# Idle TensorE matmuls before the last V block and between the transfers of wo, wo's last rows in two strips, and stores of two rows

## The chip, the cores and the metric

The kernel runs on one core of a Trainium2 chip. The metric is the device time of one execution in microseconds, as the median of several runs. A profile of one execution shows what each engine did: TensorE (PE; its weight loads apart as PEld), VectorE (DVE), ScalarE (ACT), GpSimd (POOL) and SyncE (SP), with the DMA engines.

## What is computed

One decode step for one token: attention over a cached K and V, and a gated feed-forward network, mixed by a gate. Cut to what matters:

```python
q = (x @ wq).reshape(1, 1, 32, 128)           # x: 512 values
k, v = each of 8 cached heads (32768 x 128) repeated for 4 query heads
p = softmax(q k^T * 128 ** -0.5)
a = (p v).reshape(1, 1, 4096) @ wo            # wo: 4096 x 512
b = (silu(x @ w_gate) * (x @ w_up)) @ w_down  # 1792 wide
g = sigmoid((x * gate_w).sum())
out = g * a + (1 - g) * b                     # 512 values
```

All inputs are bfloat16. K and V are 64 MB each and are read once.

## The kernel before

**Tiling.** G is 8 cached heads, with HPG = 4 query heads each. The 32768 positions of a head fall into NB = 2 blocks of 16384; a block of K or of V is one page of SBUF, 128 partitions by 128 rows by 128 values, 4 MB. Four pages hold two K and two V blocks (`PG_K`, `PG_V`); a fifth, `PG_X`, holds wq first and wo (32 rows of 512 per partition, seen as `wo_v`) later.

**The main loop on TensorE** (L518) runs G + 1 times. In iteration i, for each block b, `emit_k` transposes the K block of head i (L392, into the PSUM tiles `pst`, copied to `ktT` by VectorE at L671) and computes its scores (L404); `emit_v` multiplies the V block of head i - 1 with the exponentials that ScalarE wrote (L448). A V block is 32 matmuls of 512 columns and 16 output rows; they go to four strips of 32 columns of the array in turn (`32 * c`), so that four stand side by side. `emit_reduce` (L430) adds up what the previous head left in `acc`. The iterations' bounds are told by `pe.If`, so the last iteration has no K part: it does V block 0 of the last head, waits for V block 1 (page 3) and does it, and then runs `emit_end`.

**The end** (`emit_end`): the sums of the exponentials (L483), the last `emit_reduce` as soon as ScalarE has copied `ps_o` to `acc` (L560), then the down projection (14 rows of `wd`) by `emit_wide`: one matmul of 512 columns and one output row per row of the weight, in four strips of `ps_w` (L460). VectorE meanwhile scales and transposes the attention output (L700, L707), TensorE permutes it (L498), and VectorE copies it to `O2` (L709). Then the 32 rows of wo follow, in pieces cut at `WO_CUTS = [0, 8, 18, 26, 31, 32]`, each with a semaphore of its own transfer. The first 18 rows (`WIDE`) are `emit_wide` again. After piece 1 VectorE copies the four strips of `ps_w` to `part` (L711). The later rows use `emit_rows`: four matmuls of 128 columns each, one for each quarter of the output, to partitions 0, 32, 64 and 96 of `ps_c` (L471). After piece 2 `emit_rows` takes `part` with a column of ones at four partitions (`sel4`) as weights, which adds up the strips. At the end VectorE casts `ps_c` to `res_row` (L713), and SyncE and ScalarE store two quarters each, one DMA per quarter (`store`, L206).

**The order of transfers** is written out by hand on SyncE's queue: K and V pages as they come free (L298 to L302 and L281), V block 0 of the last head, wo's piece 0, V block 1 of the last head, `wd`, then wo's pieces 1 to 4 (L319). GpSimd waits for the stores at the end.

**Constants.** VectorE makes `sel4` from `ident` near the start, each step chained on a semaphore (`dchain`); TensorE waits for `N_SEL` of these before the main loop.

Of the kernel before, what the change touches and what calls it, by code (L numbers as in the profile page):

```python
# [6 lines left out]
ALU = mybir.AluOpType  # L7
AX = mybir.AxisListType
BF16 = mybir.dt.bfloat16
# [4 lines left out]
def bass_gated_mix__gqa_block_cached__swiglu_ffn__decode_kernel(  # L14
# [39 lines left out]
    STEP = 16  # L54
# [1 line left out]
    SCALE = float(DH) ** -0.5  # L56
    assert UPG == STEP == 4 * HPG and UPP % NKT == 0 and UPP % NST == 0
    assert KC * H * DH <= PAGE and 2 * KC * F <= PAGE and WOJ * NOUT <= PAGE
    WO_CUTS = [0, 8, 18, 26, 31, 32]
    WIDE = WO_CUTS[2]  # L60
    OC = NOUT // 128

    RQ = 4
    N_SEL = 12
    NSTRIP = 4
    assert RQ * HPG <= 32 and RQ * DH == 512

    PG_K = (0, 2)
# [5 lines left out]
    with ExitStack() as es:  # L74
# [35 lines left out]
        sem_dve_oT1 = S_("s_dve_oT1")  # L110
        sem_dve_oT2 = S_("s_dve_oT2")
        sem_dve_O2 = S_("s_dve_O2")
        sem_dve_row = S_("s_dve_row")
        sem_psw = S_("s_psw")
        sem_pe_w = S_("s_pe_w")
# [48 lines left out]
        nbias = T("nbias", [128, G, HPG], FP32)  # L164
        esum = T("esum", [128, G, NB, HPG], FP32)
        esum2 = T("esum2", [128, G, HPG], FP32)
        sel4 = T("sel4", [128, 16], FP32)
        acc = T("acc", [128, RQ, DH], FP32)
        oT = T("oT", [128, (G + 2) * STEP], FP32)
        rS = T("rS", [128, H], FP32)  # L170
# [1 line left out]
        oTs = T("oTs", [128, H], BF16)  # L172
        O2a = T("O2a", [128, WOJ], BF16)
        O2 = T("O2", [128, WOJ], BF16)
        part = T("part", [128, NOUT], FP32)
        res_row = T("res_row", [128, 128], BF16)

# [15 lines left out]
        ps_e = pst[0][:, 0:512]  # L193
        ps_c = pst[1][:, 0:512]
        ps_w = pst[0][:, 512:1024]

        def row_view(p):
            return page[:, p, :].rearrange("p (r d) -> p r d", d=DH)
# [3 lines left out]
        wo_v = page[:, PG_X, 0 : WOJ * NOUT].rearrange("p (j n) -> p j n", j=WOJ)  # L202

        def store(eng, k):
            for c in (2 * k, 2 * k + 1):
                eng.dma_start(  # L206
                    out[0, :, 128 * c : 128 * (c + 1)], res_row[32 * c : 32 * c + 1, :]
                ).then_inc(sem_out, 16)

        with nc.Block("main") as block:  # L210
            @block.gpsimd
            def _(pool):
                pool.memset(ones_bf[:, :], 1.0).then_inc(sem_const, 1)
                pool.memset(ones_f[:, :], 1.0).then_inc(sem_const, 1)
                npool = [0]

                def chain(ins):
                    ins.then_inc(sem_pool, 1)
                    npool[0] += 1
                    pool.wait_ge(sem_pool, npool[0])  # L220

                chain(pool.memset(ident[:, :], 0.0))
                pool.affine_select(
                    out=ident[:, :],
                    in_=ident[:, :],
                    compare_op=ALU.not_equal,
                    fill=1.0,
                    base=0,
                    pattern=[[-1, 128]],
                    channel_multiplier=1,  # L230
                ).then_inc(sem_ident, 1)
                chain(pool.memset(ident_f[:, :], 0.0))
                pool.affine_select(
                    out=ident_f[:, :],
                    in_=ident_f[:, :],
                    compare_op=ALU.not_equal,
                    fill=1.0,
                    base=0,
                    pattern=[[-1, 128]],
                    channel_multiplier=1,  # L240
                ).then_inc(sem_ident, 1)
                chain(pool.memset(perm[:, :, :], 0.0))
                for e in range(2):
                    pool.affine_select(
                        out=perm[:, e, :],
                        in_=perm[:, e, :],
                        compare_op=ALU.not_equal,
                        fill=1.0,
                        base=-e,
                        pattern=[[0, 2], [-2, 64]],  # L250
                        channel_multiplier=1,
                    ).then_inc(sem_ident, 1)
                pool.iota(
                    colidx[:, :],
                    pattern=[[1, 128]],
                    base=0,
                    channel_multiplier=0,
                    allow_small_or_imprecise_dtypes=True,
                ).then_inc(sem_iota, 1)
                pool.iota(  # L260
                    kf[:, :],
                    pattern=[[1, 1]],
                    base=0,
                    channel_multiplier=1,
                    allow_small_or_imprecise_dtypes=True,
                ).then_inc(sem_iota, 1)
                pool.wait_ge(sem_dve_gpart, 1)
                pool.partition_all_reduce(gtot[:, :], gpart[:, :], 128, ReduceOp.add).then_inc(
                    sem_gtot, 1
                )  # L270
                for g in range(G):
                    pool.wait_ge(sem_pmax, STEP * (g + 1))
                    pool.partition_all_reduce(  # L273
                        gmax[:, g, :], pmax[:, g * STEP : g * STEP + HPG], 128, ReduceOp.max
                    ).then_inc(sem_gmax, 1)
                pool.wait_ge(sem_out, 64)

            @block.sync
            def _(sp):
# [54 lines left out]
            def _(pe):  # L334
# [132 lines left out]
                    )  # L467

                def emit_rows(lhs, rhs, first, last):
                    for oc in range(OC):  # L470
                        ins = pe.matmul(  # L471
                            ps_c[32 * oc : 32 * oc + 1, 0:128],
                            lhs,
                            rhs[:, oc * 128 : (oc + 1) * 128],
                            start=first,
                            stop=last,
                            skip_group_check=True,
                        )
                    return ins

                def emit_end():
                    pe.wait_ge(sem_dve_esum2, 1)
                    pe.matmul(  # L483
                        ps_e[:, 0:H],
                        ones_f[:, :],
                        esum2[:, :, :].rearrange("p g h -> p (g h)"),
                        start=True,
                        stop=True,
                    ).then_inc(sem_pe_S, 1)
                    emit_reduce((G + 1) * STEP)  # L490
                    pe.wait_ge(sem_dve_tT, 1)
                    pe.wait_ge(sem_ld_wd, 16)
                    pe.wait_ge(sem_psw, 1)
                    for j in range(FC):
                        emit_wide(wd, tT, j, j < NSTRIP, False)
                    pe.wait_ge(sem_dve_oT2, 1)
                    pe.wait_ge(sem_dve_pm, 1)
                    pe.matmul(  # L498
                        ps_m[:, M_O0 : M_O0 + WOJ], pmat[:, :], O2a[:, :], start=True, stop=True
                    ).then_inc(sem_pe_O2, 1)  # L500
                    pe.wait_ge(sem_dve_O2, 1)
                    for k, s in enumerate(sem_wo):
                        pe.wait_ge(s, 16)
                        for j in range(WO_CUTS[k], WO_CUTS[k + 1]):
                            if j < WIDE:
                                ins = emit_wide(wo_v, O2, j, False, j >= WIDE - NSTRIP)
                            else:
                                ins = emit_rows(
                                    O2[:, j : j + 1], wo_v[:, j, :], j == WIDE, j == WOJ - 1
                                )  # L510
                        if k == 1:
                            ins.then_inc(sem_pe_w, 1)
                        if k == 2:
                            pe.wait_ge(sem_dve_w, 1)
                            emit_rows(sel4[:, 0:1], part[:, :], False, False)
                    ins.then_inc(sem_pe_sum, 1)

                with pe.Fori(0, (G + 1) * STEP, STEP) as i:  # L518
                    for b in range(NB):
                        with pe.If(i < G * STEP):  # L520
                            emit_k(i, b)
                        with pe.If(i > 0):
                            emit_v(i, b)
                    with pe.If(i > (G - 1) * STEP):
# [48 lines left out]
            def _(dve):  # L573
# [39 lines left out]
                )  # L613
                dve.tensor_copy(pmat[:, :], pmat_f[:, :]).then_inc(sem_dve_pm, 1)
                dve.wait_ge(sem_ident, 1)
                dchain(dve.tensor_copy(sel4[:, :], ident[:, 0:16]))
                for c in range(1, NSTRIP):
                    dchain(
                        dve.tensor_tensor(
                            sel4[:, :], sel4[:, :], ident[:, 32 * c : 32 * c + 16], ALU.add  # L620
                        )
                    )
                assert ndc[0] == N_SEL + 1
# [83 lines left out]
                dve.transpose(O2a[:, :], oTs[:, :]).then_inc(sem_dve_oT2, 1)  # L707
                dve.wait_ge(sem_pe_O2, 1)
                dve.tensor_copy(O2[:, :], ps_m[:, M_O0 : M_O0 + WOJ]).then_inc(sem_dve_O2, 1)  # L709
                dve.wait_ge(sem_pe_w, 1)  # L710
                dve.tensor_copy(part[:, :], ps_w[:, :]).then_inc(sem_dve_w, 1)  # L711
                dve.wait_ge(sem_pe_sum, 1)
                dve.tensor_copy(res_row[:, :], ps_c[:, 0:128]).then_inc(sem_dve_row, 1)  # L713


# [26 lines left out]
```

## Time and profile before

| what | us |
|---|---|
| median of 3 runs | 353.63 (353.47 to 353.99) |
| the profiled execution's own time | 354.17 |
| its span, from the first instruction to the last | 352.4 |
| last matmul group ends, cast to `res_row` starts | 349.96, 349.99 |
| stores are issued from | 350.31 |
| TensorE busy | 269.4 (76%) |
| VectorE busy | 178.5 (51%) |
| mean DMA rate over the span | 421 GB/s |

A row of the profile names an engine, a line of the kernel (L448 is line 448) and an operation with its output and inputs; "x32" is the number of instructions, "128x512" partitions by elements. "PEclk" is the share of the full TensorE clock that was granted. A wait is put down to what ended it. The chain of work follows what ended last back from the end of the span. TensorE's matmuls overlap, and their ends are modelled, so lengths of single ones hold their way through the array as well as their columns.

### The profile page before, as it was taken

The numbers are of one execution on the slowest core, as the hardware profiler recorded it, in microseconds if no ns is written. First come the engines' busy times: TensorE is split into PE (matmuls) and PEld (weight loads), VectorE is DVE, ScalarE is ACT, GpSimd is POOL, SyncE is SP. The second block draws the span as 40 slices with busy tenths as digits, with TensorE's granted clock in tenths as the row PEclk, the third lists the DMA queues.
The fourth block names the chain that finished last, engine by engine and source line by source line (L and its number), as shares of the span: only waits on it lengthen the run. The fifth ranks groups of instructions, "written<-read, shape, count | busy, mean of one in ns | idle before, by whom it ended". The sixth has DMA issues, their size and how long they took to land.

```text
span 352.4 us, 8926 instructions
## 1 busy us (share of the span) xinstructions
PE 269.4 (76%) x4005; PEld 231.1 (66%) x4005; DVE 178.5 (51%) x204; ACT 32.3 (9%) x148; POOL 5.8 (2%) x24
## 2 busy tenths in 40 slices
PE   0446986997999959697798959795997859695376
PEld 0446976976687949395786849494966759593033
DVE  0310967655683938266562828274655728193001
ACT  1000000400120040002100040003000030004000
POOL 0200000000000000000000000000000000000000
PEclk9999988789898998769885978679887969898656
DMA  8999999999999999999999999999999999999994
GB/s 331 411 432 426 445 433 416 430 424 450 420 432 424 450 421 428 424 450 420 432 424 450 420 432 424 450 420 432 424 450 420 432 424 450 420 432 420 439 402 163
DMA packets 5924, 148.23 MB, mean 421 GB/s; under 512 B 666, under 2 KB 796, under 8 KB 924
## 3 DMA queue, kind: packets, MB, share of 16 engines
q1 hardware_dynamic: 5912, 148.12, 98.2%
q8 instruction: 6, 0.10, 0.1%
q14 instruction: 2, 0.02, 0.0%
q10 hardware_dynamic: 4, 0.00, 0.0%
HBM read 148.11 MB, written 0.00 MB: 420 GB/s over the span
## 4 chain that ended last, share of the span: by engine, by line
DMA 58%; PE 36%; DVE 3%; issue 1%; SPq 1%; ACT 0%; ACTq 0%
DMA page<-in_A_k_cache_dram 54%; PE pst L392 25%; PE ps_sc L404 6%; DMA page<-in_A_v_cache_dram 5%; PE ps_o L448 3%; DVE ktT L671 3%; PE pst L460 1%; PE ps_m L430 1%; PE pst L471 1%; SPq L302 0%; ACT acc L560 0%; SPq L298 0%; SPq L299 0%; DVE res_row L713 0%; SPq L300 0%
## 5 line engine op out<-in xcount | busy, mean ns | idle before, releaser
L671 DVE COPY ktT<-pst 128x2048 bf16<-128x2048 bf16 x128 | 155.8, 1224 | 106.6 <-PE pst L392 99.6
L392 PE MATMUL pst<-ident_f,page 128*128 128x128 f32 x1024 | 158.2, 311 | 41.5 <-DMA page<-in_A_k_cache_dram 39.2
L392 PEld LDWEIGHTS pst<-ident_f,page 128*128 128x128 f32 x1024 | 134.6, 161 | 53.0 <-DMA page<-in_A_k_cache_dram 47.0
L404 PEld LDWEIGHTS ps_sc<-qcur,ktT 128*128 128x128 bf16 x2048 | 67.1, 97 | 11.4 <-DVE ktT L671 10.0
L404 PE MATMUL ps_sc<-qcur,ktT 128*128 128x8 bf16 x2048 | 67.9, 166 | 8.6 <-DVE ktT L671 8.6
L448 PE MATMUL ps_o<-page,ET 128*16 128x512 bf16 x512 | 43.0, 495 | 7.9 <-DMA page<-in_A_v_cache_dram 7.9
L448 PEld LDWEIGHTS ps_o<-page,ET 128*16 128x16 bf16 x512 | 13.5, 105 | 26.7 <-issue 20.3
L539 ACT ACTIVATE nbias<-gmax 128x4 f32<-128x4 f32 x8 | 1.6, 205 | 263.2 <-POOL gmax L273 263.2
L548 ACT ACTIVATE ET<-ps_sc,nbias 128x128 bf16<-128x128 f32 x64 | 24.1, 553 | 0.7
L548 ACT ACTIVATION_READ_ACCUMULATOR ET<-ps_sc,nbias 128x1 f32 x64 | 18.1, 282 | 0.0
L676 DVE TENSOR_REDUCE pmaxf<-ps_sc 128x4 f32<-128x512 f32 x16 | 11.1, 692 | 11.5 <-PE ps_sc L404 11.5
L430 PE MATMUL ps_m<-sel,acc 128*128 128x4 f32 x72 | 11.4, 282 | 3.7 <-ACT acc L560 3.7
L430 PEld LDWEIGHTS ps_m<-sel,acc 128*128 128x128 f32 x72 | 10.8, 229 | 4.3 <-ACT acc L560 4.3
L340 PE MATMUL ps_m<-ones_bf,x_row 1*128 1x1 bf16 x4 | 0.3, 172 | 13.6 <-DMA gw_row<-in_gate_w_dram 13.6
L377 PE MATMUL ps_m<-xT,page 128*128 128x1 bf16 x112 | 6.9, 198 | 4.2 <-DMA page<-in_B_w_up_dram 4.2
L377 PEld LDWEIGHTS ps_m<-xT,page 128*128 128x128 bf16 x112 | 6.8, 159 | 4.3 <-DMA page<-in_B_w_up_dram 4.3
L340 PEld LDWEIGHTS ps_m<-ones_bf,x_row 1*128 1x128 bf16 x4 | 0.2, 114 | 13.6 <-DMA gw_row<-in_gate_w_dram 13.6
L694 DVE RECIPROCAL rS<-pst 128x32 f32<-128x32 f32 x1 | 0.4, 358 | 15.3 <-PE pst L483 15.3
L273 POOL PARTITION_ALL_REDUCE gmax<-pmax x8 | 3.0, 372 | 291.7 <-DVE pmax L678 291.7
L560 ACT ACTIVATE acc<-ps_o 128x512 f32<-128x512 f32 x8 | 5.2, 650 | 17.0 <-PE ps_o L448 17.0
L585 DVE CAST xT<-ps_m 128x4 bf16<-128x4 f32 x1 | 0.2, 163 | 12.5 <-PE ps_m L340 12.5
L353 PE MATMUL ps_m<-xT,page 128*128 128x1 bf16 x128 | 3.6, 165 | 0.3 <-DVE gwT L586 0.3
(68 smaller groups left out, 33.6 us busy)
## 6 DMA issues: line engine op xcount, KB each, us to landing
page<-in_A_k_cache_dram SPq DMA_DIRECT2D x16, 4096.0 KB, 26.9
page<-in_A_v_cache_dram SPq DMA_DIRECT2D x16, 4096.0 KB, 31.2
page<-in_A_wq_dram SPq DMA_DIRECT2D x1, 4096.0 KB, 12.4
page<-in_A_wo_dram SPq DMA_DIRECT2D x2, 1024.0 KB, 24.7
page<-in_B_w_gate_dram SPq DMA_DIRECT2D x1, 1792.0 KB, 15.7
page<-in_B_w_up_dram SPq DMA_DIRECT2D x1, 1792.0 KB, 20.5
wd<-in_B_w_down_dram SPq DMA_DIRECT2D x1, 1792.0 KB, 20.5
page<-in_A_wo_dram SPq DMA_DIRECT2D x1, 1280.0 KB, 23.1
```

The lines of the kernel that those rows point to most:

```text
L353: ins = pe.matmul(ps_m[:, M_Q0 + h : M_Q0 + h + 1], wq_v[:, c, h * DH : (h + 1) * DH], xT[:, c : c + 1], start=(c == 0), stop=(c == KC - 1),)
L377: ins = pe.matmul(ps_m[:, base + j : base + j + 1], wgu[:, w, c, :].rearrange("d (p j) -> d j p", j=FC)[:, j, :], xT[:, c : c + 1], start= ...
L392: ins = pe.transpose(pst[u % NST][:, k * 128 : (k + 1) * 128], kv[:, n * 128 : (n + 1) * 128], ident_f[:, :],)
L404: ins = pe.matmul(ps_sc[b][:, col : col + 2 * HPG], kt[:, k, e, :], qcur[:, e, :], start=(e == 0), stop=(e == 1),)
L430: ins = pe.matmul(ps_m[:, M_P0 : M_P0 + HPG], acc[:, q, :], sel4[:, q * HPG : (q + 1) * HPG], start=(q == 0), stop=(q == RQ - 1),)
L448: ins = pe.matmul(ps_o[32 * c : 32 * c + RQ * HPG, :], ET[:, n : n + RQ, :].rearrange("p n h -> p (n h)"), view[:, k * RQ : (k + 1) * RQ, ...
L460: return pe.matmul(ps_w[32 * c : 32 * c + 1, :], vec[:, j : j + 1], w[:, j, :], start=first, stop=last, skip_group_check=True,)
L471: ins = pe.matmul(ps_c[32 * oc : 32 * oc + 1, 0:128], lhs, rhs[:, oc * 128 : (oc + 1) * 128], start=first, stop=last, skip_group_check=True,)
L548: act.activation(ET[:, b * R : (b + 1) * R, h], sc[:, h, :], ACT.Exp, bias=nbias[:, g, h : h + 1], scale=SCALE, accum_out=esum[:, g, b, h ...
L560: act.activation(acc[:, :, :].rearrange("p q d -> p (q d)"), ps_o[:, :], ACT.Copy).then_inc(sem_acc, STEP)
L671: dve.tensor_copy(ktT[:, u % NKT, :], pst[u % NST][:, :].bitcast(BF16)).then_inc(sem_cp, 1)
L676: dve.tensor_reduce(pmaxf[:, b, :], sc, AX.X, ALU.max).then_inc(sem_pmax, 4)
```

## The change

Before V block 1 of the last head TensorE runs 18 matmuls (`NWARM`) of the identity with 512 columns of `ktT` into a part of `pst` that nobody reads (`ps_d`); they stand in a loop with two in its body, within a `pe.If` that is true in the last iteration alone. Six such matmuls stand behind wo's piece 1 and two behind piece 2 (`NGAP`). wo's cuts move to 30 and 32 at the end, and rows 18 to 25 become wide (`WIDE` is 26). `part` is copied after piece 2, and its sum starts the accumulation in `ps_c`. The rows from 26 on and `part` use two strips of two output rows: the weight is two columns wide, one of them zero (`O2z`, `sel5`), so quarter `oc` lands in row `oc % 2` of strip `oc // 2`. `res_row` then has its rows at partitions 0, 1, 32 and 33, and each queue stores two of them with one DMA. VectorE zeroes `O2z` and a column of `sel5` at the start and fills `O2z` with two copies after `O2`.

```diff
-    WO_CUTS = [0, 8, 18, 26, 31, 32]
-    WIDE = WO_CUTS[2]
+    WO_CUTS = [0, 8, 18, 26, 30, 32]
+    KW = 2
+    WIDE = WO_CUTS[KW + 1]
+    NWARM = 18
+    NGAP = [0, 6, 2]
...
-    N_SEL = 12
+    N_SEL = 13
     NSTRIP = 4
+    RPS = 2
...
+        ps_d = pst[1][:, 512:1024]
...
         def store(eng, k):
-            for c in (2 * k, 2 * k + 1):
-                eng.dma_start(
-                    out[0, :, 128 * c : 128 * (c + 1)], res_row[32 * c : 32 * c + 1, :]
-                ).then_inc(sem_out, 16)
+            n = RPS * 128
+            eng.dma_start(
+                out[0, 0, n * k : n * (k + 1)].rearrange("(c n) -> c n", c=RPS),
+                res_row[32 * k : 32 * k + RPS, :],
+            ).then_inc(sem_out, 16)
...
-                    for oc in range(OC):
-                        ins = pe.matmul(
-                            ps_c[32 * oc : 32 * oc + 1, 0:128],
-                            lhs,
-                            rhs[:, oc * 128 : (oc + 1) * 128],
-                            start=first,
-                            stop=last,
-                            skip_group_check=True,
-                        )
+                    for e in range(RPS):
+                        for k in range(OC // RPS):
+                            oc = RPS * k + e
+                            ins = pe.matmul(
+                                ps_c[32 * k : 32 * k + RPS, 0:128],
+                                lhs(e),
+                                rhs[:, oc * 128 : (oc + 1) * 128],
+                                start=first and e == 0,
+                                stop=last and e == RPS - 1,
+                                skip_group_check=True,
+                            )
                     return ins
+
+                def emit_idle(n):
+                    for _ in range(n):
+                        pe.matmul(ps_d, ident[:, :], ktT[:, 0, 0:512], start=True, stop=True)
+
+                def emit_warm():
+                    with pe.Fori(0, NWARM, 2):
+                        emit_idle(2)
...
                                 ins = emit_rows(
-                                    O2[:, j : j + 1], wo_v[:, j, :], j == WIDE, j == WOJ - 1
+                                    lambda e: O2z[:, j - WIDE, e, :],
+                                    wo_v[:, j, :],
+                                    False,
+                                    j == WOJ - 1,
                                 )
-                        if k == 1:
+                        if k < KW:
+                            emit_idle(NGAP[k])
+                        if k == KW:
                             ins.then_inc(sem_pe_w, 1)
-                        if k == 2:
+                            emit_idle(NGAP[k])
                             pe.wait_ge(sem_dve_w, 1)
-                            emit_rows(sel4[:, 0:1], part[:, :], False, False)
+                            pe.wait_ge(sem_dve_oz, RPS)
+                            emit_rows(lambda e: sel5[:, 1 - e : 3 - e], part, True, False)
                     ins.then_inc(sem_pe_sum, 1)
...
+                        if b == NB - 1:
+                            with pe.If(i > (G - 1) * STEP):
+                                emit_warm()
                         with pe.If(i > 0):
                             emit_v(i, b)
...
+                dve.memset(O2z[:, :, :, :], 0.0)
+                dchain(dve.memset(sel5[:, 0:1], 0.0))
...
+                for e in range(RPS):
+                    dve.tensor_copy(
+                        O2z[:, :, e, e], ps_m[:, M_O0 + WIDE : M_O0 + WOJ]
+                    ).then_inc(sem_dve_oz, 1)
                 dve.wait_ge(sem_pe_w, 1)
                 dve.tensor_copy(part[:, :], ps_w[:, :]).then_inc(sem_dve_w, 1)
                 dve.wait_ge(sem_pe_sum, 1)
-                dve.tensor_copy(res_row[:, :], ps_c[:, 0:128]).then_inc(sem_dve_row, 1)
+                dve.tensor_copy(res_row[0 : 32 + RPS, :], ps_c[0 : 32 + RPS, 0:128]).then_inc(sem_dve_row, 1)
```

More of the change, by code (lines that the diff above doesn't have):

```diff
@@ L112, in bass_gated_mix__gqa_block_cached__swiglu_ffn__decode_kernel @@
         sem_dve_O2 = S_("s_dve_O2")
+        sem_dve_oz = S_("s_dve_oz")
         sem_dve_row = S_("s_dve_row")
@@ L166, in bass_gated_mix__gqa_block_cached__swiglu_ffn__decode_kernel @@
         esum2 = T("esum2", [128, G, HPG], FP32)
-        sel4 = T("sel4", [128, 16], FP32)
+        sel5 = T("sel5", [128, 17], FP32)
+        sel4 = sel5[:, 1:17]
         acc = T("acc", [128, RQ, DH], FP32)
@@ L174, in bass_gated_mix__gqa_block_cached__swiglu_ffn__decode_kernel @@
         O2 = T("O2", [128, WOJ], BF16)
+        O2z = T("O2z", [128, WOJ - WIDE, RPS, RPS], BF16)
         part = T("part", [128, NOUT], FP32)
@@ L275, in _ @@
                     ).then_inc(sem_gmax, 1)
-                pool.wait_ge(sem_out, 64)
+                pool.wait_ge(sem_out, 32)
             @block.sync
@@ L615, in _ @@
                 dve.wait_ge(sem_ident, 1)
-                dchain(dve.tensor_copy(sel4[:, :], ident[:, 0:16]))
+                dve.memset(O2z[:, :, :, :], 0.0)
+                dchain(dve.memset(sel5[:, 0:1], 0.0))
+                dchain(dve.tensor_copy(sel4, ident[:, 0:16]))
                 for c in range(1, NSTRIP):
@@ L619, in _ @@
                         dve.tensor_tensor(
-                            sel4[:, :], sel4[:, :], ident[:, 32 * c : 32 * c + 16], ALU.add
+                            sel4, sel4, ident[:, 32 * c : 32 * c + 16], ALU.add
                         )
```

## The prediction

> **What bounds the kernel now.** The page's part 2 came first: the DMA engines are busy in all of the span but its last slice, so until the last V block has landed only transfers count. Then the chain of work in order of time (columns: start us, length us, what), for the last block:
>
> ```profile
> 318.58 1.86 PE ps_o L448 x32
> ...
> 320.46 16.60 DMA page<-in_A_v_cache_dram
> 337.06 0.12 issue
> 337.18 3.62 PE ps_o L448 x32
> ...
> 341.52 1.87 PE ps_m L430 x8
> 343.39 1.80 PE pst L460 x11
> ...
> 345.61 1.98 PE pst L460 x17
> 347.59 2.37 PE pst L471 x53
> 349.96 0.02 issue
> 349.99 0.29 DVE res_row L713
> ```
>
> The same 32 matmuls of a V block take 1.86 us at 318.58 and 3.62 us at 337.18. From 337.18 on the chain is TensorE's, at half speed. Transfers are a second bound just beneath it: by the landing records wo's rows 8-17 are there at 344.44, 18-25 at 346.95, 26-30 at 348.52 and row 31 at 348.87. TensorE ends 1.09 us after that.
>
> The clock I read from the table by stretches, cut at the clock's own steps, which lie 3.413 us apart or multiples of it (columns: stretch, length, PE busy and matmuls begun, granted clock, DMA share, GB/s):
>
> ```profile
> 315.67:319.08 3.41, 2.87 (x73) 1.00 1.05 452
> 319.08:322.50 3.42, 1.34 (x28) 1.00 0.87 374
> 322.50:325.91 3.41, 1.98 (x12) 0.50 1.03 435
> 325.91:329.32 3.41, 3.41 (x32) 0.50 1.07 459
> 329.32:332.74 3.42, 0.00 (x0) 1.00 1.00 431
> 332.74:336.15 3.41, 0.00 (x0) 0.50 0.90 384
> 336.15:339.56 3.41, 2.38 (x24) 0.50 0.98 417
> 339.56:342.98 3.42, 3.24 (x21) 0.50 1.01 425
> 342.98:346.39 3.41, 3.13 (x25) 0.50 0.96 392
> 346.39:349.80 3.41, 3.41 (x78) 0.50 0.23 91
> ```
>
> Each row's work sets the next row's clock. Two rows look wrong until one counts streaming and not presence: 339.56 and 342.98 hold L430, whose f32 matmuls stream four columns and otherwise load weights. I counted columns streamed (four strips side by side as one; 4096 fill a step at half clock) for every step of the span. All steps with 3147 or fewer are followed by half clock, all with 3227 or more by full, whatever the clock within. That is **about 2.65 us of streaming at half clock or 1.33 us at full**. Row 319.08 has 1.34 us busy, its last round's drain included, and misses it.
>
> Last, the timeline of the end (start, length, instruction, idle before):
>
> ```profile
> 347.95 0.69 DVE L711 COPY part<-pst 128x512 f32<-128x512 f32 x1 [2.39 <-PE pst L460]
> 348.70 0.61 PE L471 MATMUL pst<-part,sel 128*1 128x128 f32 x8
> 349.08 0.86 PE L471 MATMUL pst<-page,O 128*1 128x128 bf16 x24
> 350.31 0.57 SPq L206 DMA_DIRECT2D out_dram<-res_row  x2
> 350.31 0.76 ACTq L206 DMA_DIRECT2D out_dram<-res_row  x2
> ```
>
> The sum is made against this execution: 354.17 us with a span of 352.4; the median is 353.63. The clock's steps need not lie so in every run, so the sum is made for other positions too.
>
> **The idle run before the last V block.** 18 matmuls of 512 columns over the whole array, no such row in the trace. Below: 0.058 us each, a thirty-second of a V block at full clock (one strip of four), 1.0 us in all. Above: 0.495 us, the mean length of an L448 matmul alone, 8.9 us. I take a round of four strips, which streams 512 columns over the array: 1.72/8 = 0.215 us at full clock, 0.427 at half. The loop adds a branch for each two; the sequencer's branch at L518 lasts 0.21 us with some 0.15 around it and ran while V matmuls streamed, so it hides behind the pair's 0.43. The run begins when the other V block's stream ends (329.15) and, nearly all at full clock, ends at 329.15 + 3.95 = **333.1**. Then TensorE waits until 337.18. Step 332.74-336.15 holds 0.4 us of it, under 1.33: the clock drops at 336.15, and the V block takes 3.6 us as before. The run is an engine's idle time and costs nothing, but buys nothing either.
>
> The row at 329.32, nothing streamed and the clock halved at its end, agrees with the Trainium skill, "TensorE: Matmul & The Clock Gate", section "What's actually happening", which has half clock after one idle window. Read strictly, that would spare the V block here, as step 332.74-336.15 is not wholly idle; the sum would then be that of the kept clock below. Row 319.08, with 1.34 us of work and a drop, speaks against that reading, and the row decides.
>
> **The idle matmuls within wo.** In this position of the steps everything up to the first wo matmul stays: 345.61. The 18 wide ones as before, 18 x 0.107 (0.427 over four strips), to 347.53. Six idle: 6 x 0.427 = 2.56, to 350.09, less 0.15 for the clock's rise at 349.80. Before they lay where rows ran; now rows 18-25, landed at 346.95, stand behind them. This is the dearest term.
>
> **Rows 18-25 wide, `part` later.** Eight wide matmuls replace 32 row matmuls (1.17 us in the chain): 8 x 0.054 at full clock, to 350.4. But `part` now waits for them: 0.3 to the copy's start, 0.69 the copy (L711's row), 0.05 to TensorE: 351.4. The two idle ones fit under it. In before the copy lay beside those 32 row matmuls; that cover is gone.
>
> **Two strips in place of four.** `part`'s 8 f32 passes took 0.38 us start to start at half clock over four strips; over two, 0.77 at half, 0.43 at full (256 columns' time each, two at once). The 24 remaining row matmuls: 12 rounds of 128 columns, 0.64 us at full clock, 1.28 at half, against 0.64 in before. With 0.2 from the stream's end to the cast: 351.4 + 0.43 + 0.64 + 0.2 = 352.7, against 349.99: **+2.7**.
>
> **Stores.** One DMA per queue goes. In before the packets of the first two end at 351.06 and 351.08, the last at 351.57: **-0.47** (bounds: 0, if two rows take a queue as long as two DMAs; -0.5). The cast, 34 rows by 128 columns, keeps its 0.29.
>
> **The rest.** On VectorE a zeroing and a chained one are added at 16.4; 0.85 us of idle follow before 18.00, and the row nearest is 0.2 each. Two copies into O2z, about 0.19 each (L709's row), lie in the 2.39 us that it waits for L460. One more branch per half iteration on TensorE, 0.07 to 0.21 us, delays a V block by at most that; the next load issued (320.46) waits behind transfers that last until 327.3. wo's cut moves 128 KB between two transfers back to back; the last landing stays 348.87.
>
> **Sum.** Here +2.7 - 0.47 = +2.2: span 354.6, time 356.4. Moving the steps through their 3.413 us with the same rows gives, for the cast's start, before 349.3 to 350.1 (middle 349.55; such a spread of 0.8 suits the 0.5 between the runs shown) and after:
> - about a quarter: the V block itself fills a step, full clock near 340 to 343.4, then a drop while rows 8-17 are awaited; the six idle ones are sped up from about 347: 350.2 to 350.5.
> - about a third: part of the V block at full clock, O2 at 344.4 to 345.1, six idle ones at half clock to 348.8: 351.5.
> - the rest: as above, 352.0 to 352.7.
>
> Against before's middle, less 0.47: +0.1 to +0.5, +1.4, +2.0 to +2.7. The middle position gives +1.4: 353.63 + 1.4 = **355.0 us**. Without the store's gain 355.5.
>
> **Rivals.**
> 1. *The clock is kept.* If one idle matmul costs over some 0.4 us, or the threshold differs, the run lasts past 336 and the V block runs at full clock. For it: the upper bound, which would even hold the V block back by 1 us to 338.2, yet run it in 1.86. Against: the V rounds, and branches that hid. Then the chain is rows 18-25's landing: 347.07 + 0.43 + 0.3 + 0.75 + 0.43 + 0.64 + 0.2 = 349.8, not before's 349.55 in the middle. Less 0.47: -0.2, 353.4. No change.
> 2. *Faster.* The same, and before's runs are mostly as the profiled one (349.99): -0.2 - 0.47 = -0.7, or -1.2 if the last landing's 348.87 + 0.5 could set the end: 352.4 to 352.9. It decides only where `part`'s copy comes sooner than worked out; the wait for rows 18-25 speaks against it.
> 3. *Idle matmuls all at half clock to the end*, rows too: 352.7 + 0.64 + 0.4 less 0.47: 356.8.
>
> **How the numbers follow.** Forecast (late by the idle matmuls within wo) 0.58, of it a tenth inside 0.2%; rival 1 0.24; rival 2 0.12; rival 3 0.06. With 0.2% (0.71 us) as what a measurement can tell from no change: slower 0.58, same 0.30, faster 0.12. The range leaves out rival 3 and most of rival 2: 353.0 to 356.3; the forecast's own is 353.8 to 356.3.
>
> **What would show it.** Right: the idle run ends near 333, a stretch under 1.33 us follows and the clock is 0.50 within the V block or soon after; six idle matmuls of about 0.43 us with wo's rows 18-25 landed and waiting; `part`'s copy after 348; one packet end per queue about 0.75 us after the cast. Wrong: an idle run that lasts to 336 or later, full clock from 337 to 349, and a cast before 349.9.

## The result and the profile after

The changed kernel takes **355.10 us** (median of 22 runs, 353.36 to 357.12) against 353.65 (22 runs, 353.10 to 354.71): 1.0042 times before, 95% interval 1.0024 to 1.0060. So it is slower by 0.4%, and the runs lie over 3.8 us where before's lie over 1.6. They fall into three groups: six from 353.4 to 353.7, eight from 354.3 to 355.5, eight from 356.2 to 357.1.

The profiled execution (355.33 us, span 353.5) is of the middle group. Its chain in order of time, from wo's piece 1 on (columns: start us, length us, what; L469 the wide matmuls, L494 the idle ones, L482 the rows in two strips):

```profile
344.56 1.44 PE pst L469 x10
346.00 2.67 PE pst L494 x6
348.68 0.76 PE pst L469 x7
...
349.46 0.70 DVE part L745
...
350.21 1.29 PE pst L482 x32
...
351.52 0.28 DVE res_row L747
```

Where before's chain had rows of wo, six matmuls that nobody reads stand for 2.67 us, and wo's rows 18-25, landed at 347.02 in this execution, wait behind them until 348.68. The cast starts at 351.52 in place of 349.99.

The table by stretches, cut at the clock's steps of this execution (stretch, length, PE busy and matmuls begun, granted clock, DMA share, GB/s):

```profile
328.56:331.98 3.42, 3.42 (x21) 0.50 0.98 422
331.98:335.39 3.41, 2.99 (x14) 1.00 0.95 409
335.39:338.80 3.41, 1.55 (x32) 1.00 0.98 414
338.80:342.22 3.42, 2.46 (x32) 1.00 0.98 413
342.22:345.63 3.41, 2.73 (x25) 0.50 1.00 412
345.63:349.04 3.41, 3.41 (x16) 0.50 0.43 168
```

Here the clock rose late (331.98), so the idle run, begun at 329.90, ran at half clock for its first 2 us, ended at 334.97, and carried the full clock up to 338.80; the V block's own 1.55 us in the step from 335.39 kept it to 342.22. The V block, from 337.25, took 1.90 us at full clock. Then came a step in which TensorE waited for ScalarE, loaded f32 weights and did the down projection: 2.46 us busy, but little streaming, and the clock was at half from 342.22 on. The gain before it bought nothing, since wo's rows 8-17 landed at 344.51 in any case; the loss behind it fell on the six idle matmuls.

The stores, from the timeline (start, length, instruction), issued 0.31 us after the cast's start:

```profile
351.83 0.27 SPq L214 DMA_DIRECT2D out_dram<-res_row  x1
351.84 0.60 ACTq L214 DMA_DIRECT2D out_dram<-res_row  x1
```

From the cast's start to the end of the span it is 2.0 us against 2.37: 0.37 gained.

### The profile page after: what moved, and what is told of

Read it like the earlier page. It is cut to its first block, busy times and chain, and to the rows that moved or that the text cites. A ratio compares the mean times of both kernels' runs of the same rounds, so it can differ in the third digit from the quotient of the medians.

```text
span 353.5 us, 8961 instructions
## 1 busy us (share of the span) xinstructions
PE 274.7 (78%) x4007; PEld 232.5 (66%) x4007; DVE 179.0 (51%) x208; ACT 32.1 (9%) x148; POOL 5.8 (2%) x24
## 4 chain that ended last, share of the span: by engine, by line
DMA 60%; PE 35%; DVE 3%; SPq 1%; issue 1%
DMA page<-in_A_k_cache_dram 54%; PE pst L401 25%; DMA page<-in_A_wo_dram 6%; PE ps_sc L413 6%; DVE ktT L701 3%; PE ps_o L457 2%; PE pst L494 1%; PE pst L469 1%; PE pst L482 0%; PE ps_m L439 0%; SPq L311 0%; DVE part L745 0%; SPq L334 0%; SPq L307 0%; SPq L290 0%
## 5 line engine op out<-in xcount | busy, mean ns | idle before, releaser
L457 PE MATMUL ps_o<-page,ET 128*16 128x512 bf16 x512 | 40.4, 472 | 2.4 <-DMA page<-in_A_v_cache_dram 2.3
L386 PE MATMUL ps_m<-xT,page 128*128 128x1 bf16 x112 | 6.9, 198 | 3.8 <-DMA page<-in_B_w_up_dram 3.8
L494 PE MATMUL pst<-ktT,ident 128*128 128x512 bf16 x26 | 8.4, 483 | 0.0
L494 PEld LDWEIGHTS pst<-ktT,ident 128*128 128x128 bf16 x26 | 2.8, 116 | 6.1 <-issue 4.8
```

Of the source, the lines that this page charges most:

```text
L386: ins = pe.matmul(ps_m[:, base + j : base + j + 1], wgu[:, w, c, :].rearrange("d (p j) -> d j p", j=FC)[:, j, :], xT[:, c : c + 1], start= ...
L457: ins = pe.matmul(ps_o[32 * c : 32 * c + RQ * HPG, :], ET[:, n : n + RQ, :].rearrange("p n h -> p (n h)"), view[:, k * RQ : (k + 1) * RQ, ...
L494: pe.matmul(ps_d, ident[:, :], ktT[:, 0, 0:512], start=True, stop=True)
```

## The experiments

Theory T is the prediction's: the clock follows what the step before streamed; the change puts the idle run too early to hold it to the end, and then pays, at half clock, for the idle matmuls within wo and for the rows' new form. R1, nearest to the prediction's own name for its forecast, puts the whole loss on the six idle matmuls, R2 on the rows and the copy of `part`, with the clock of no account.

**Stores alone** (`e1_stores`), on before, whose quarters lie at partitions 0, 32, 64, 96:

```diff
-            for c in (2 * k, 2 * k + 1):
-                eng.dma_start(
-                    out[0, :, 128 * c : 128 * (c + 1)], res_row[32 * c : 32 * c + 1, :]
-                ).then_inc(sem_out, 16)
+            eng.dma_start(
+                out[0, 0, 256 * k : 256 * (k + 1)].rearrange("(c n) -> c n", c=2),
+                res_row[64 * k : 64 * k + 33 : 32, :],
+            ).then_inc(sem_out, 16)
...
-                pool.wait_ge(sem_out, 64)
+                pool.wait_ge(sem_out, 32)
```

> Before with the two-row stores alone: one DMA per queue takes the rows at partitions 0 and 32, or 64 and 96. From the trace of after (cast's start to the end of the span 2.0 us, 2.37 in before) 0.37 less: 353.3. A rival in which a two-row DMA costs what two DMAs do expects no change, 353.65.

Measured: 354.14 us against 353.60 in the same session, ratio 1.0013 (1.0004 to 1.0022): slower, which neither expected. The timeline of its end:

```profile
350.18 0.58 SPq L205 DMA_DIRECT2D out_dram<-res_row  x1
350.19 1.40 ACTq L205 DMA_DIRECT2D out_dram<-res_row  x1
```

One DMA over partitions 64 and 96 takes ScalarE's queue 1.40 us to issue, against 0.60 over partitions 32 and 33 in the changed kernel and 0.76 for two DMAs in before. From the cast's start to the end of the span it is 2.69 us. So the change's 0.37 belongs to two rows on neighbouring partitions, which only the two strips provide; it can't be had from before's layout by this form.

**Without the idle matmuls within wo** (`e2_no_gap`: `NGAP = [0, 0, 0]`) and **without any** (`e3_no_idle`: the loop before the V block goes as well).

> After without the six and the two idle matmuls between wo's pieces; the 18 before the V block stay. Theory T (loss from both: the idle ones on the path, and the late copy of part with two strips, each dear only at half clock): without the idle ones the clock is at half for what follows, so only the top falls (the slowest run from 357.1 to about 356.2) and the median goes from 355.1 to about 354.8. Rival R1 (the six idle matmuls are the whole loss): 2.3 us less in the slow positions, median near 353.2. Rival R2 (rows and copy are the whole loss): 355.1 as after.

> After without any idle matmul, the late copy of part, the two strips and the stores kept. T and R2: still about 1.1 to 1.3 over before, 354.8. R1: below before by the stores, 353.3. If the loop before the V block matters by itself, this differs from the kernel that lacks the gaps alone; T expects the same within 0.2.

Measured: 354.93 (353.82 to 355.79), ratio 1.0037 (1.0021 to 1.0053), and 354.56 (354.08 to 354.81), 1.0027 (1.0017 to 1.0038). R1 falls: without one idle matmul the kernel is still about 1.0 us over before. The medians do not tell T's 354.8 from R2's 355.1. What speaks against R2 as the whole is that the slow group of 356.2 to 357.1 is gone: none of these 16 runs is over 355.8, and none is under 353.8, so the fast group is gone as well. That the two kernels differ from each other is not shown; their intervals overlap. Nor is the idle matmuls' net cost clear of noise, since the change's own 1.0024 to 1.0060 overlaps with both. In the profiles the cast starts at 350.99 and 350.97 here, against 351.52 in the change's first profile: the 2.67 us of idle matmuls on that path are worth some 0.5 us net. The clock in the first one's profile went as the prediction worked it out for before's position: the step from 332.47 held 0.16 us of the idle run's end, half clock followed from 335.88 to 349.53, and the V block took 3.59 us.

What is left in the second is seen in its timeline:

```profile
348.63 1.02 PE L482 MATMUL pst<-part,sel 128*2 128x128 f32 x8 [0.80 <-DVE part L742]
349.43 1.50 PE L482 MATMUL pst<-page,O2z 128*2 128x128 bf16 x24
```

In before the same groups took 0.61 and 0.86, at half clock too but for the last 0.14 us: two matmuls stand side by side where four did. And TensorE waited 0.80 us for the copy of `part`, beside which before had 32 row matmuls.

**The idle matmuls on before's rows** (`e4_idle_on_before`: before's cuts and four strips, the strided stores of the first experiment, 18 idle matmuls before the V block, 6 after piece 1, 2 after piece 2).

> Before's rows, cuts and four strips, with the two-row stores and all of the change's idle matmuls (18 before the V block, 6 and 2 between wo's pieces). T: spread as wide as after's but lower, 353.0 to 355.4, median about 354.1 (worked out over the positions of the clock's steps: 0.4 over before). R1: as after, 355.1. R2: as the stores alone, 353.3.

Measured: 353.93 us, ratio 1.0028 (1.0008 to 1.0049), but over 353.25 to 356.36: six runs of twelve from 353.25 to 353.73, four from 355.49 to 356.36. T's median of 354.1 was near, but it had counted the stores as a gain, which they are not, and its range ended 1.0 us too low. R2 asked for the stores alone (354.14, none above 354.96) and R1 for 355.1 in the median. With the idle matmuls a run comes out low or up to 3 us higher. The profile is of a low run (353.30), and three rows of its table by stretches show how the clock went:

```profile
332.80:336.21 3.41, 0.38 (x1) 1.00 0.90 384
336.21:339.63 3.42, 2.81 (x28) 0.50 0.99 421
339.63:343.04 3.41, 2.93 (x33) 1.00 1.00 420
```

The idle run ended too early here too (333.21), and half clock followed at 336.21. But 2.81 us of the V block then fell into one step at half clock, full clock came back at 339.63, before the down projection, and stayed to the end.

**A longer idle run** (`e5_run36`: `NWARM = 36`, all else as changed).

> After with 36 idle matmuls before the V block in place of 18, nothing else. T (what counts is whether the step ahead of the V block and those behind it stream 1.33 us at full clock): the run lasts to 336.9 or later, the V block is at full clock in every position. Then two groups of runs: six in ten with full clock to the end, near 353.4 (0.2 under before), four in ten that lose it after the V block and pay the six idle matmuls, near 355.0. Median 353.4 to 354. Rival R2 (rows and late copy are the loss, the clock is not): as the kernel without idle matmuls, 354.6, in one group. Rival R4 (a longer run only holds the V block back, by 0.5 to 1 us): 355.6 to 356.1.

Measured: 354.30 us, the middle of two groups: six runs from 353.19 to 353.53 and six from 355.08 to 356.45; ratio 1.0016 (0.9996 to 1.0036). The two groups are T's, the upper one 0.1 to 1.4 us over its place; T had six runs in ten in the lower, so its median of 353.4 to 354 was missed. R2's single group and R4's times are not seen. The profile is of the upper group: V block at full clock, then the down projection's step, half clock from 342.98, and the six idle matmuls in 2.67 us.

**Copy early again, idle matmuls where each step needs them** (`e6_early_copy_run36`):

```diff
-    KW = 2
+    KW = 1
     WIDE = WO_CUTS[KW + 1]
-    NWARM = 18
-    NGAP = [0, 6, 2]
+    NWARM = 36
+    NGAP = [4, 4]
```

> After with part copied after piece 1 again (rows 18 on by the two-strip rows), 36 idle matmuls before the V block, 4 after wo's piece 0 and 4 after piece 1. T: every step from the V block to the end streams enough in nearly every position, so the clock is full throughout and the spread between runs, 3.8 us in after, falls to some 0.3; the end is set by the last landing: 353.1, 0.5 under before, and faster than both kernels. R2: about 354.2, as the two strips alone. R4: 354 or more.

Measured: 353.31 us over 353.01 to 353.58, ratio 0.9990 (0.9980 to 1.0000). The spread of 3.8 us has become 0.6. The table by stretches of its profile, cut at its steps:

```profile
333.99:337.41 3.42, 3.42 (x18) 1.00 0.93 395
337.41:340.82 3.41, 3.00 (x40) 1.00 0.99 416
340.82:344.23 3.41, 2.86 (x32) 1.00 1.00 416
344.23:347.65 3.42, 3.18 (x35) 1.00 0.81 326
347.65:351.06 3.41, 1.78 (x54) 1.00 0.03 12
```

Four idle matmuls after piece 0 lift the step of the down projection, four after piece 1 the next; both stand in waits for wo's landings. The clock is full to the end, which this execution's late last landing (349.24) then sets. The time was expected 0.2 lower. The long run also held the V block back a little: it ended at 337.70, and the block, landed at 337.43, began at 337.85 and not some 0.12 us after its landing; that is a cost of R4's kind, 0.3 us, and here the later landings hid it.

**Copy early, no idle matmuls** (`e7_early_copy_no_idle`: `KW = 1`, no loop, `NGAP = [0, 0, 0]`).

> After without idle matmuls and with part copied after piece 1: what is left are two strips and two-row stores. T: 0.4 to 0.6 over before, 354.1, against 354.6 for the kernel with the late copy: the late copy costs about 0.4, the two strips at half clock about 1 less the stores' 0.37. If the late copy were the whole loss of rows: 353.3.

Measured: 355.08 us (353.07 to 356.70), ratio 1.0030 (1.0006 to 1.0054), and its profiled execution 356.70. The expectation missed by 1 us. Why this execution was late is in its trace, which is at half clock throughout the end:

```profile
348.90 1.02 PE L482 MATMUL pst<-part,sel 128*2 128x128 f32 x8 [0.79 <-DVE part L742]
349.71 3.13 PE L482 MATMUL pst<-page,O2z 128*2 128x128 bf16 x56
```

With `KW = 1` in the changed code the wait for the copy stands ahead of piece 2's rows, so nothing covers it; and 56 row matmuls in two strips at half clock cost 3.13 us. Rows 18-25 as eight wide ones would take 8 x 0.107 = 0.86 at half clock (an estimate from before's 18 wide ones, 0.427 for four). From the copy's start to the cast it is 4.73 us here and 3.09 in the profile of the late copy without idle matmuls, so with two strips at half clock the change's late copy is the better by some 0.8, the eight wide ones counted in. Over all runs the two are not told apart (1.0030 and 1.0027): five of the runs here lie under 353.8, below every run of that other kernel (354.08). The spread of 3.6 us, without one idle matmul, shows too that it is not the idle matmuls alone that spread the runs.

**Idle matmuls alone** (`e8_idle36_on_before`: before with 36 idle matmuls before the V block, 4 after piece 0, 4 after piece 1).

> Before as it is, four strips and one-row stores, with the idle matmuls alone: 36 before the V block, 4 after piece 0, 4 after piece 1. T: full clock from the V block on, cast at 349.27, set by the last landing: 0.3 under before, 353.3, with a spread of some 0.3. If transfers hid all of it: 353.6 as before. R4: 354 or more.

Measured: 353.33 us (353.02 to 354.00), ratio 0.9990 (0.9980 to 1.0001). At T's place; that it is under before is at the edge of its interval. Its profiled execution has full clock from 329.39 to 349.87, and its cast starts 0.3 us after the last landing, 1.1 us in before.

**Late copy, four strips** (`e9_late_copy_four_strips`: before with the cuts `[0, 8, 18, 26, 30, 32]`, rows 18 to 25 wide and `part` copied after piece 2; no idle matmuls, one-row stores).

> Before with the change's cuts, rows 18 to 25 wide and part copied after piece 2, but four strips, one-row stores and no idle matmul. It stands between before and the change without idle matmuls (354.6). If the two strips are what costs there (the f32 passes of part and 24 row matmuls at half clock, 1.02 and 1.28 us against 0.39 and 0.64 in four strips, less 0.37 for the stores): 0.9 under that kernel, 353.6, no change against before. If the late copy costs it: 354.6 to 354.9 still.

Measured: 354.11 us against 353.74, ratio 1.0014 (1.0003 to 1.0026). Between the two answers: the late copy costs some 0.4 us, and the two strips less their stores about as much again, 0.4 to 0.6 of the 1.0 of the kernel without idle matmuls. The expectation's price for the strips set groups at half clock (1.02) against groups at full (0.39); at half clock in both it is 1.02 against 0.61.

**One row behind the last cut** (`e10_one_row_last`: the sixth experiment with the last cut at 31).

> The fastest kernel so far (part copied after piece 1, two strips, two-row stores, 36 idle matmuls before the V block, 4 after piece 0, 4 after piece 1) with wo's last cut at 31 in place of 30, so that four matmuls and not eight stand behind the last landing. T: 0.1 less than with the cut at 30, 353.2, 0.4 under before, with a spread of some 0.5 that the landings alone make. If a shorter row of 1 KB per partition lands later than two rows by as much: no difference.

Measured: 353.19 us (352.89 to 353.56) against 353.74, ratio **0.9985** (0.9976 to 0.9994). It is faster than both kernels, with the change's idle matmuls at other places, its two strips and its stores, but with `part` copied after piece 1 and rows 18 to 25 no longer wide. That the cut itself gives 0.1 is within the intervals of the two. Nor is this kernel told apart from before with the idle matmuls alone (0.9980 to 1.0001).

**Two single executions**: the change again (`e11_after_again`), and with 16 idle matmuls before the V block (`e12_run16`).

> The change once more, for a look at another position of the clock's steps. If the idle run ends more than 3.4 us before the V block is there, or the step that holds its end has under 1.33 us of it, T expects the V block at half clock in part or in whole, the six idle matmuls at 0.427 us each behind wo's landed rows 18 to 25, a cast start of 352.0 to 352.7 and a time of 356.2 to 357.1; in the positions like the first profile 355.3, and in the fast group 353.5 with full clock from the V block to the end.

> The change with 16 idle matmuls before the V block in place of 18: the run ends 0.43 us earlier. T: the same three groups of positions, the slow one a little wider; one execution shows one of them: 353.5, 355.3 or 356.2 to 357.1. A time outside these would speak against T.

Measured: 354.80 and 356.21 us. In the first the idle run ended near 333.9, the next step was idle, the V block took 3.57 us at half clock and, filling a step, brought full clock back at 340.82: the quarter of positions that the prediction had as its first. The clock fell again at 344.23, at the end of the down projection's step, and the six idle matmuls took 2.12 us on the path. So the way was as worked out, but the cast started at 350.99 where the prediction had 350.2 to 350.5, and the time lies 0.7 us over that group's 354.1, among the middle ones. This execution's own expectation had 356.2 to 357.1 for a V block at half clock; it did not allow for the block winning the clock back, and missed. The second is the slow position. Its timeline and chain, one fence for each:

```profile
328.67 3.19 PE L494 MATMUL pst<-ktT,ident 128*128 128x512 bf16 x14
336.96 3.59 PE L457 MATMUL ps_o<-page,ET 128*16 128x512 bf16 x32 [5.10 <-DMA page<-in_A_v_cache_dram]
```

```profile
345.39 2.30 PE pst L469 x14
347.69 2.07 PE pst L494 x6
349.76 0.56 PE pst L469 x8
...
350.34 0.70 DVE part L745
...
352.40 0.28 DVE res_row L747
```

The idle run is over at 331.9, 5.1 us before the V block begins; the V block takes before's 3.6 us, the first wide matmul starts where before's does, and the cast is at 352.40, where the prediction had 352.7.

## Why the prediction was right

The time was forecast at 355.0 and is 355.10, and the parts of the way that the prediction gave are seen in the profiles: the clock lost around the idle run, idle matmuls on the path, the late copy and the two strips. That it agrees to 0.1 us is in part luck. The runs fall into three groups of six, eight and eight over 3.8 us, and the median is where it is because the middle group lies in the middle. Its steps:

- **The idle run ends too early.** Shown in the kernels with 18 and 16 at several positions (end near 332.6 without the gaps, 333.9, 331.9; half clock from 335.88, 337.41 and 335.36) and by the long run, whose end at 336.5 was followed by full clock. In the first profile of the change it ended at 334.97, as its start was at half clock, and the whole V block was at full clock. There the prediction's sign of a stretch under 1.33 us after the run failed; it had only part of a V block so. Its second group has `O2` ready at 344.4 to 345.1 and the cast at 351.5. Here `O2` was ready at 343.1, wo's rows 8-17 were awaited until 344.51, and the cast came at 351.52: the same time by another wait.
- **The idle matmuls on the path.** 0.427 us each was taken, 2.56 for six; the chain shows 2.67 where all ran at half clock, 2.07 where the step rose within them. But the prediction named its forecast after this term and called it the dearest, and that is more than the runs show. Without one idle matmul the median is still 1.0 us over before, out of 1.45; what the idle ones add to it is not clear of noise. What the kernels with the late copy do show is that the slow and the fast group come with the idle matmuls.
- **`part` later and two strips.** From `part`'s start to the cast 1.27 was worked out at full clock, 1.31 is measured (350.21 to 351.52). At half clock the two groups cost 1.02 and 1.50 in place of 0.61 and 0.86.
- **Stores.** -0.47 was taken, -0.37 came: ScalarE's issue takes 0.60 us for two rows, 0.51 for the first of one row. The term was mis-sized by a fifth. The sign of one packet end per queue 0.75 us after the cast was misread from before's rows: there the first packets end 0.75 us after the issue, 1.07 after the cast; in the change each queue's two packets end 1.1 to 1.2 us after the cast.
- **The groups.** About a quarter near 353.7 to 354.1, a third at 355.0, the rest at 355.6 to 356.3 were worked out. Six of 22 came at 353.4 to 353.7, eight at 354.3 to 355.5, eight at 356.2 to 357.1. Three things failed here. The execution that went the first group's way (354.80) lies 0.7 us over its place. The runs at 353.4 to 353.7, which is rival 1's time, are not explained by a profile of the change; in the profile of before's rows with the idle matmuls (353.30) the clock was not kept, as rival 1 has it, but lost and won back by the V block itself. That the change's runs at 353.4 to 353.7 go the same way is not shown. And the slow group is 0.6 to 0.8 above its place. Its mechanism is seen at 356.21; the rest is not. V's landing differs by up to 0.74 us between the profiled executions of all kernels (336.69 to 337.43), which can move the end by as much; that is argued, no profile shows a run of 357.
- **The threshold.** "3147 or fewer, 3227 or more" holds for before's profile and was too sharp. A count of the same kind over all fourteen profiles has steps of up to 3395 columns followed by half clock and steps from 2764 by full; in the profile of the change one of 3350 (147.66) by half and one of 3230 (202.27) by full. So it is a band, 1.15 to 1.41 us of streaming at full clock. The count itself is coarse, since some matmuls are missing from the traces (the one without the gaps has 9 of its 18 idle ones).
- **Sums.** The middle group is 351.5 - 349.55 - 0.47 = +1.48 by its own terms, not +1.4: 355.1. Rival 3's 356.8 counts from the profiled cast (349.99); counted from 349.55 like the groups it is 357.3.

What the prediction did not see is that the idle matmuls can be made to pay a little: where they hold the clock in every step to the end, the time is 353.19 with the strips and stores (spread 0.7 us) and 353.33 with before's rows (spread 1.0). That the strips and stores add to it is not shown.

## What to carry to other kernels

Before adding work that keeps an engine's clock up, find the clock's steps in the profile and count what streams in each step between that work and the end: one thin step behind it (here the one with the f32 weight loads and the down projection, 2.46 us busy and half clock after) undoes it. Put the idle work only into waits, in amounts that fit at half clock too, and never ahead of data that has landed. And where a time depends on where such steps fall, which differs from execution to execution (a step began at 329.32 in before's profile, at 331.98 in the change's and at 330.58 in its second), forecast the groups and compare many runs; a single execution of this kernel could have said 353.4 or 357.1.

## What was not expected of the hardware

- Issuing one DMA of two rows takes ScalarE's queue 0.60 us when the rows lie on neighbouring partitions (32 and 33) and 1.40 when they lie 32 apart (64 and 96); SyncE's queue 0.27 (0 and 1) and 0.58 (0 and 32).
- The last landing of the inputs varies between executions of kernels that load the same inputs in the same order: 348.50 to 349.24 us in fourteen profiles. A gain of 0.2 us at the end is not seen in one run.
